# A four-layer transformer backward kernel: operands fetched one part ahead at the stage joints, some transposes moved to TensorE, one reordering on VectorE

## Chip, cores and metric

The kernel runs on one core of one Trainium2 chip, in one launch. The metric is the device time of that launch in microseconds (us), lower is better. A core has TensorE (PE in the profile, its weight loads PEld), VectorE (DVE), ScalarE (ACT), GpSimd (POOL), the sync engine SP, which here only issues DMAs, and 16 DMA engines.

## What is computed

Four residual layers alternate between linear attention (A, layers 0 and 2) and attention in a sliding window of 256 (B, layers 1 and 3), with the same weights for both A layers and for both B layers. The kernel returns the output x4 and, by back-propagation of `grad_out`, the gradients of x and of four weight matrices. Cut to what matters:

```python
def A(x, wqkv, wo):                       # x: [1, 2048, 640], 32 heads of 20
    q, k, v = split(x @ wqkv)             # wqkv: [640, 1920]
    pq, pk = phi(q), phi(k)               # phi(t) = (t + 1 if t > 0 else exp(t)) + 1e-6
    kv, z = pk^T v, sum(pk)               # per head
    return (pq kv) / (pq z + 1e-6) @ wo
def B(x, wqkv, wo):
    s = mask(q k^T / sqrt(20))            # 0 <= i - j < 256
    return softmax(s) v @ wo
x = x + A(ln(x)); x = x + B(ln(x)); x = x + A(ln(x)); x = x + B(ln(x))
out, vjp = jax.vjp(f, A_x, A_wqkv, A_wo, B_wqkv, B_wo)
return out, *vjp(grad_out)
```

## The kernel before

Rows are cut into 16 tiles of 128; the 640 columns are 5 tiles of 128; the 32 heads form 8 groups of 4. After the forward part (until about 875 us) come these stages:

- `seg_attention_bwd(3)` (about 875 to 1205 us): the backward pass of the softmax of layer 3, over 128 units (group, row tile). A unit makes scores twice (L905), e = exp (ACT, L919), dS = e times dP (DVE, two halves, L939), needs dS transposed, and five units later forms dq, dk, dv by products (L965), evicted into `dqkv_o` (L998) and stored to the DRAM tensor `dqkv` by POOL. Half 0 of dS is transposed by a DMA (`self.tr`, from SP's queue), half 1 by TensorE (`flip`, L949) through the one PSUM buffer `tp`, evicted by ACT and DVE in turn.
- `seg_dense_bwd(3)`, part 1 (to about 1349): per row of layer 3, dh = dqkv W^T (L773, needs `dqkvT`, the DMA-transposed row), LayerNorm backward on ACT and DVE (`ln_bwd`, L776 to L790), which ends with the residual gradient `car` (L790); then for linear-attention layer 2, car transposed (L730), dO = g Wo^T (L738), the products `do_o` on POOL (L753) and their row sums `do_s` on DVE (L755), dN, its transposes, dq (`dq_t`, L1256), and sums over all rows in two PSUM banks ("bands"). `close_A_bwd` turns the bands into the block-diagonal matrix `dmbd`, cleared before by POOL (L1151), and its transpose `dmbdT`.
- part 2 (to about 1499): per row dk and dv from `pk_ld`, `pkT`, `vT` (a load and two DMA transposes; `dkdv`), the products with WA^T, LayerNorm backward, and the slab dO of layer 1 (`B_do`).
- `seg_attention_bwd(1)` (to about 1967), with the weight gradients of layers 3 and 2 filled in; `seg_dense_bwd(1)`, part 1 (to about 2111) and part 2 (to about 2219).
- `wgrad` for layer 1 and then 0 (to the end): four jobs of 4, 2, 4 and 2 chunks of columns. Each output tile sums 16 matmuls (L1388), and `wg_o` (L1394) adds the part of the earlier layers, `wg_pt`.

The order of the work: the program is written row by row as a list of small functions with an offset in rows (`plan`); a scheduler orders instructions of each engine by dependences and priorities, and a pool's number of buffers bounds how far it runs ahead. `self.queue` and `queue2` hold loads that `drip` puts out on SP a few at a time, kept in the order of the program; SP issues in order, so what stands behind a DMA that waits, waits too. `behind` adds an order between two instructions without a semaphore. The loads of dense backward (`rows_in`, `tr`), the dS transposes, wgrad's loads and its output stores are all in SP's queue; other stores go out on POOL (`flush`). Lines that set the offsets:

```python
plan = ((fetch, 2), (dh0, 0), (dh1a, 0), (flip_g, -1), (dh1b, 0), (flip_dN, -2), (dO, -1), (flip_dq, -3), (dq_band, -2))  # part 1
plan = ((fetch, 4), (fetch2, 2), (dh0, 0), (flip_dkv, 1), (dh1a, 0), *tail[:1], (dh1b, 0), *tail[1:2], (dkdv, 2), *tail[2:])  # part 2
for s in range(-4, TT + 2):
```

Of the kernel before, what the change touches and what calls it, by code (L numbers as in the profile page):

```python
# [16 lines left out]
P = 128  # L17
DH = 20
# [5 lines left out]
class Kern:  # L24

    def __init__(self, ctx, tc, x0, A_wqkv, A_wo, B_wqkv, B_wo, grad_out, outs):
# [14 lines left out]
        self.queue, self.queue2, self.stores = [], [], []  # L41
        self.x0, self.grad_out = x0, grad_out
# [121 lines left out]
    def load_w(self, pool, kind, name):  # L164

        D, DT = self.D, self.DT
        if name == "W":
            t = pool.tile([P, DT, self.QT], BF, name=f"W{kind}")
            src = self.Wqkv[kind].rearrange("(kt p) n -> p kt n", p=P)
            pairs = [(t[:, k, c:c + D], src[:, k, c:c + D]) for c in range(0, self.QT, D) for k in range(DT)]  # L170
# [572 lines left out]
    def do_scaled(self, l, tt, ps, o, dst, pw):  # L743
# [11 lines left out]
        nc.vector.tensor_reduce(out=s, in_=self.hv(t), axis=AX.X, op=ALU.add, negate=True)  # L755
# [20 lines left out]
    def ln_bwd(self, l, tt, ps, hn, g, pw):  # L776
# [13 lines left out]
        nc.vector.scalar_tensor_tensor(out=self.car[:, tt, :], in0=u, scalar=ab[:, 0:1], in1=g,  # L790
                                       op0=ALU.add, op1=ALU.add)
# [65 lines left out]
    def seg_attention_bwd(self, l, fill, end):  # L857
# [5 lines left out]
        JL, PL, OH, WG = 5, 1, 4, 12 * DH  # L863
        units = [(g, b) for g in range(G) for b in range(TT)]
        slabs, e_of, ds_of, dsT_of = {}, {}, {}, {}
        self.att_outs, self.att_step = {}, 0
        with ExitStack() as st:
# [63 lines left out]
            def dscore(u, half, ps):  # L931
# [10 lines left out]
                if half == 0:  # L942
                    self.tr(dsT_of[u][:, 0:2 * nkt, :], ds_of[u][:, 0:2 * nkt * P])

            def flip(u):
                nb = 2 * span(units[u][1])[1]
                tp = ps_o.tile([P, 1024], BF, name="tp")
                for i in range(nb):
                    nc.tensor.transpose(tp[:, i * P:(i + 1) * P], ds_of[u][:, (nb + i) * P:(nb + i + 1) * P],  # L949
                                        self.ident)  # L950
                dst = dsT_of[u][:, nb:2 * nb, :].rearrange("p i q -> p (i q)")
                evac(u + 1)(dst, tp[:, 0:nb * P])
# [56 lines left out]
            n = len(units)  # L1009
            for s in range(n + JL):  # L1010
# [16 lines left out]
                if 0 <= b2 < n:  # L1027
                    dscore(b2, 1, pb)
                if bank:
                    job(s - JL, *bank)  # L1030
# [116 lines left out]
    def close_A_bwd(self, bands, pool, pt):  # L1147

        nc, D, DT, H = self.nc, self.D, self.DT, self.H
        dmbd = pool.tile([P, DT, 6 * P], BF, name="dmbd")  # L1150
        nc.gpsimd.memset(dmbd, 0.0)  # L1151
# [12 lines left out]
        return dmbd, dmbdT  # L1164
# [7 lines left out]
    def seg_dense_bwd(self, l, w, mid):  # L1172
# [5 lines left out]
        with ExitStack() as st:  # L1178
# [4 lines left out]
            dqT = pb.tile([P, DT, self.T], BF, name="dqT")  # L1183
            rows = lambda t: slice(t * P, (t + 1) * P)

            with ExitStack() as s2:
# [4 lines left out]
                WTA = WoTB = None  # L1191
                pps = self.pool(s2, "ps", 2, PSUM)
                pbd = self.pool(s2, "psb", 1, PSUM)
# [7 lines left out]
                def fetch(t):  # L1201
# [7 lines left out]
                    o[t] = self.rows_in(pl.tile([P, D], BF, name="o_ld", bufs=4), self.o_d[a][:, t, :])  # L1209
                    pq[t] = self.rows_in(pl.tile([P, D], BF, name="pq_ld", bufs=5), self.tm(sv["pq"])[:, t, :])  # L1210
# [27 lines left out]
                def dq_band(t):  # L1238
# [16 lines left out]
                    dq[t] = p1w.tile([P, D], BF, name="dq_t")  # L1255
# [4 lines left out]
                def flip_dq(t):  # L1260
                    self.flip(dq.pop(t), DT, dqT[:, :, rows(t)], pt, [nc.scalar.copy])

                plan = ((fetch, 2), (dh0, 0), (dh1a, 0), (flip_g, -1), (dh1b, 0), (flip_dN, -2), (dO, -1), (flip_dq, -3),
                        (dq_band, -2))
                for s in range(-2, TT + 3):
                    for f, d in plan:
                        if 0 <= s + d < TT:
                            f(s + d)
                    self.drip(2)
                    if s == 2:  # L1270
                        WTA = self.load_w(pb, 0, "WT")
                        WoTB = self.load_w(pb, 1, "WoT") if a > 0 else None
                dmbd, dmbdT = self.close_A_bwd(bands, pb, pt)
            mid()

            with ExitStack() as s2:
                p2 = self.pool(s2, "b2")
# [3 lines left out]
                hn, o, pk, pkT, vT, ps, gT, dkv, dkvT = ({} for _ in range(9))  # L1281
# [3 lines left out]
                def fetch(t):  # L1285
                    pk[t] = self.rows_in(pl.tile([P, D], BF, name="pk_ld"), sv["pk"][rows(t), :])
                    pkT[t] = pl.tile([P, DT, P], BF, name="pkT")
                    self.tr(pkT[t], sv["pk"][rows(t), :])
                    vT[t] = pl.tile([P, DT, P], BF, name="vT")
                    self.tr(vT[t], sv["v"][rows(t), :])  # L1290
# [6 lines left out]
                def dkdv(t):  # L1297
                    f = pw.tile([P, D], BF, name="dphi")
                    nc.vector.tensor_scalar(out=f, in0=pk.pop(t), scalar1=-1e-6, scalar2=1.0, op0=ALU.add, op1=ALU.min)
# [13 lines left out]
                    vT.pop(t), pkT.pop(t)  # L1313
# [34 lines left out]
                for s in range(-4, TT + 2):  # L1348
# [11 lines left out]
    def wgrad(self, l, pools, first=False):  # L1360

        nc, TT, D, DT, HD = self.nc, self.TT, self.D, self.DT, self.HD
        kind = l % 2
        pW, pw = pools[:2]
        jobs = [(self.hn_d[l], self.dqkv_d[l], 480, self.part[kind][0], (self.out_dWA, self.out_dWB)[kind], kind == 1),
                (self.o_d[l], self.g_d[l], HD, self.part[kind][1], (self.out_dWoA, self.out_dWoB)[kind], False)]
        for lhs_d, rhs_d, w, part, out, perm in jobs:
            lhs = pW.tile([P, TT, D], BF, name="wg_l", bufs=2)
            self.later([(lhs[:, tt, :], lhs_d[:, tt, :]) for tt in range(TT)])
            n = part.shape[1] // w  # L1370

            def load(c):
                r = pw.tile([P, TT, 480], BF, name="wg_r")
                return r, [(r[:, t:t + 2, 0:w], rhs_d[:, t:t + 2, c * w:(c + 1) * w]) for t in range(0, TT, 2)]
            rhs, pieces = load(0)
            self.later(pieces)
            if first:
                yield
            self.drip(len(self.queue), False)
            for c in range(n):  # L1380
                nxt, pieces = load(c + 1) if c + 1 < n else (None, [])
                for m in range(DT):
                    rows = slice(m * P, (m + 1) * P)
                    pt = pw.tile([P, 480], F32, name="wg_pt")
                    self.dma(pt[:, 0:w], part[rows, c * w:(c + 1) * w], nc.sync)
                    ps = pools[2].tile([P, 512], F32, name="wg")[:, 0:w]
                    for tt in range(TT):
                        nc.tensor.matmul(ps, lhsT=lhs[:, tt, rows], rhs=rhs[:, tt, 0:w],  # L1388
                                         start=(tt == 0), stop=(tt == TT - 1))
                        yield  # L1390
                        if tt % 8 == 7 and pieces:
                            self.dma(*pieces.pop(0), nc.sync)
                    o = pw.tile([P, 480], BF, name="wg_o")
                    nc.vector.tensor_add(o[:, 0:w], ps, pt[:, 0:w])  # L1394
                    if perm:
                        for h in range(w // (12 * DH)):
                            g = c * (w // (12 * DH)) + h
                            dst = out[rows, :].rearrange("r (t g c) -> r t g c", t=3, c=4 * DH)[:, :, g, :]
                            self.dma(dst, o[:, h * 12 * DH:(h + 1) * 12 * DH].rearrange("p (t c) -> p t c", t=3),
# [147 lines left out]
```

## Time and profile before

| | |
|---|---|
| time, median of 3 runs | 2412.37 us (2407.59 to 2415.21) |
| the profiled execution | 2408.5 us, of which the span is 2406.8 |
| TensorE clock granted, mean | 0.935 |
| busy: PE, DVE, ACT, POOL | 2141.7, 1550.2, 1259.9, 1156.0 us |
| DMA | 472 MB, 196 GB/s over the span |
| TensorE idle in 1205 to 1499 (dense 3) | 33.6 us |
| in 1499 to 1967 (attention 1) | 46.5 us |
| in 1967 to 2219 (dense 1) | 26.7 us |
| in 2219 to 2407 (wgrad) | 11.2 us |

The profiled execution is 3.9 us under the median. "Busy" is the time in which an engine executes; the idle times are the stretch less TensorE's busy time in it. A line of a timeline gives the start in us, the length, the engine (PEld is TensorE's weight load, SPq an issue in SP's queue), the line of the kernel, the operation with output and input, the shapes, the number of instructions drawn together and, in brackets, the idle time before them and what ended it. The granted clock is a share of full speed[...].

### The profile page before, as it was taken

To read this page: it belongs to the slowest core of one execution; us is meant where nothing else is said; L and a number is where in the kernel's file an instruction comes from. 1 tells how busy PE (TensorE), PEld (TensorE's weight loads), DVE (VectorE), ACT (ScalarE), POOL (GpSimd) and SP (SyncE) were. 2 spreads that over 40 slices of the span, in tenths; PEclk is the share of its full clock that TensorE was granted. 3 is DMA by queue.
4 is the path that set the end of the run, shared out by engine and by line. 5 is a ranking of instruction groups with operands and counts; after the bars stand their busy time and mean duration, and the time that the engine had idled before them with its cause. 6 is when DMAs were issued, how large, how long until landed. Compare 5 with 4: busy or idle time off the path is not lost. (4 is left out here: it accounts for less than half of the span.)

```text
span 2406.8 us, 68820 instructions
## 1 busy us (share of the span) xinstructions
PE 2141.7 (89%) x27566; PEld 1491.8 (62%) x27672; DVE 1550.2 (64%) x2991; ACT 1259.9 (52%) x2002; POOL 1156.0 (48%) x1791
## 2 busy tenths in 40 slices
PE   6879899879998689999989797889999979889989
PEld 4645565545555357777667575667777747657445
DVE  6657777557778558878766586556667656646112
ACT  4447777637777557777623353555666633333000
POOL 4447667656877535656533243445555533311000
PEclk9989999989999859999899898789999989989999
DMA  8599898478998798889998695999889898497797
GB/s 257 145 185 217 183 198 185 132 175 197 226 209 187 190 242 163 147 149 164 181 230 200 166 241 172 241 211 198 178 177 209 169 211 226 122 266 207 204 272 213
DMA packets 813666, 472.08 MB, mean 196 GB/s; under 512 B 609664, under 2 KB 780336, under 8 KB 813344
## 3 DMA queue, kind: packets, MB, share of 16 engines
q1 hardware_dynamic: 771152, 334.46, 67.0%
q0 software_dynamic: 42192, 133.21, 17.9%
q8 instruction: 216, 3.54, 0.6%
q14 instruction: 106, 0.87, 0.1%
HBM read 187.07 MB, written 161.19 MB: 145 GB/s over the span
## 5 line engine op out<-in xcount | busy, mean ns | idle before, releaser
L939 DVE SCALAR_TENSOR_TENSOR ds<-sp,e 128x768 bf16<-128x768 f32 (+2 forms) x512 | 462.8, 906 | 235.5 <-PE sp L905 148.9
L919 ACT ACTIVATE e<-sp 128x768 bf16<-128x768 f32 (+2 forms) x512 | 395.0, 776 | 257.4 <-PE sp L905 172.0
L418 ACT ACTIVATE e<-s 128x1024 bf16<-128x1024 f32 x360 | 365.2, 1025 | 109.2 <-PE s L412 67.2
L412 PE MATMUL s<-qbd,ring 128*128 128x512 bf16 x614 | 212.3, 388 | 7.7 <-ACT e L418 3.9
L1045 PEld LDWEIGHTS <-wg_l 128*128 128x128 bf16 x2800 | 187.3, 99 | 45.6 <-DVE wg_o L1051 14.1
L923 POOL TENSOR_SCALAR_AFFINE_SELECT e<-e 128x512 bf16<-128x512 bf16 x256 | 164.6, 643 | 94.0 <-ACT e L919 91.4
L905 PE MATMUL sp<-KT,QT 32*128 32x384 bf16 (+2 forms) x1024 | 184.8, 345 | 17.6 <-ACT e L919 10.5
L421 POOL TENSOR_SCALAR_AFFINE_SELECT e<-e 128x512 bf16<-128x512 bf16 x256 | 170.0, 666 | 54.1 <-ACT e L418 52.5
L905 PE MATMUL sp<-VT,dOT 32*128 32x384 bf16 (+2 forms) x1024 | 180.9, 341 | 10.8 <-ACT e L919 7.2
L1388 PE MATMUL wg<-wg_r,wg_l 128*128 128x480 bf16 (+1 forms) x960 | 176.8, 347 | 7.4 <-DMA out_dram<-wg_o 6.4
L1045 PE MATMUL acc<-wg_r,wg_l 128*128 128x160 bf16 x1840 | 157.4, 239 | 24.3 <-DMA wg_l<-o 7.4
L267 PE MATMUL d<-W,ln_hnT 128*128 128x320 bf16 x960 | 150.0, 304 | 28.3 <-ACT ln_hnT L732 9.6
L368 PE MATMUL d<-W,ln_hnT 128*128 128x480 bf16 x640 | 158.5, 380 | 4.0 <-DMA ln_hnT<-ln_hn 1.3
L424 POOL TENSOR_SCALAR_AFFINE_SELECT e<-e 128x512 bf16<-128x512 bf16 x224 | 150.9, 674 | 9.9 <-ACT e L418 9.1
L1388 PEld LDWEIGHTS <-wg_l 128*128 128x128 bf16 x960 | 94.5, 99 | 89.5 <-DMA out_dram<-wg_o 6.7
L773 PE MATMUL d<-WT,dqkvT 128*128 128x320 bf16 x960 | 144.4, 304 | 4.5 <-DMA dqkvT<-dqkv 4.5
L440 PEld LDWEIGHTS <-e 128*128 128x128 bf16 x2880 | 110.4, 97 | 60.5 <-POOL e L421 18.5
L927 POOL TENSOR_SCALAR_AFFINE_SELECT e<-e 128x512 bf16<-128x512 bf16 x224 | 142.8, 638 | 0.0
L267 PEld LDWEIGHTS <-ln_hnT 128*128 128x128 bf16 x960 | 93.8, 99 | 78.0 <-issue 22.5
L949 PE MATMUL tp<-ident,ds 128*128 128x128 bf16 x1440 | 135.9, 234 | 5.3 <-DVE ds L939 3.3
L440 PE MATMUL d<-v_slab,e 128*128 128x42 bf16 (+1 forms) x2880 | 115.9, 180 | 23.1 <-POOL e L421 16.1
L965 PEld LDWEIGHTS <-dsT 128*128 128x128 bf16 x2880 | 93.5, 98 | 67.5 <-issue 46.4
(204 smaller groups left out, 4554.0 us busy)
## 6 DMA issues: line engine op xcount, KB each, us to landing
qkvT<-ring POOLq DMA_DIRECT2D x32, 512.0 KB, 5.1
dqkv<-dqkv_o POOLq DMA_DIRECT2D x64, 240.0 KB, 4.2
wg_r<-dqkv SPq DMA_DIRECT2D x64, 240.0 KB, 4.6
hn<-ln_hn SPq DMA_DIRECT2D x64, 160.0 KB, 3.0
qk<-qk_flat POOLq DMA_DIRECT2D x64, 160.0 KB, 3.9
qk_r<-qk SPq DMA_DIRECT2D x32, 320.0 KB, 4.5
hn_ld<-hn SPq DMA_DIRECT2D x64, 160.0 KB, 3.6
dqkv<-dkv_t POOLq DMA_DIRECT2D x32, 320.0 KB, 4.0
```

The lines of the kernel that those rows point to most:

```text
L267: nc.tensor.matmul(ps, lhsT=hnT[:, k, :], rhs=W[:, k, ci * HD:(ci + 1) * HD], start=(k == 0), stop=(k == self.DT - 1))
L368: nc.tensor.matmul(ps, lhsT=hnT[:, k, :], rhs=W[:, k, ci * 480:(ci + 1) * 480], start=(k == 0), stop=(k == self.DT - 1))
L412: nc.tensor.matmul(ps[:, i, :], lhsT=self.ring_at(ring, 1, kt)[:, g, :], rhs=self.qbd[b % 2][:, g, :, :], start=True, stop=True)
L418: nc.scalar.activation(e[:, 0:i + 1], ps[:, 0:i + 1], ACT.Exp, scale=self.c_att)
L421: nc.gpsimd.affine_select(out=ev, in_=ev, compare_op=ALU.is_ge, fill=0.0, base=0, pattern=[[0, 4], [1, P]], channel_multiplier=-1)
L440: nc.tensor.matmul(ov[:, h % 16:h % 16 + w, :], lhsT=ev[i][:, hh, :], rhs=v[:, h:h + w, 0:DH + 1], start=(i == 0), stop=(i == nkt - 1), sk ...
L905: nc.tensor.matmul(ps[:, j, 0:nkt * P], lhsT=slabs[g][ta][r0:r0 + HP, b * P:(b + 1) * P], rhs=slabs[g][tb][r0:r0 + HP, k0 * P:(k0 + nkt) * P],
L919: nc.scalar.activation(ev[:, 2 * half:2 * half + 2], ps[:, :, 0:nkt * P].rearrange("p h (i k) -> p h i k", k=P), ACT.Exp, scale=c_att)
L923: nc.gpsimd.affine_select(out=ev[:, :, nkt - 1, :], in_=ev[:, :, nkt - 1, :], compare_op=ALU.is_ge, fill=0.0, base=0, pattern=[[0, 4], [-1 ...
L939: nc.vector.scalar_tensor_tensor(out=dv[:, hs], in0=ps[:, :, 0:nkt * P].rearrange("p h (i k) -> p h i k", k=P), scalar=c_att, in1=ev[:, hs ...
L1045: x = self.nc.tensor.matmul(ps[:, 0:w], lhsT=lhs(t), rhs=rhs(t), start=(t == 0), stop=(t == self.TT - 1), skip_group_check=True)
L1388: nc.tensor.matmul(ps, lhsT=lhs[:, tt, rows], rhs=rhs[:, tt, 0:w], start=(tt == 0), stop=(tt == TT - 1))
```

## The change

It has eight parts.

1. `do_s` (L755) is ordered behind the last written `car` (`self.car_ins`, L790).
2. The pieces of W are loaded in the column order D, 2D, 0 in place of 0, D, 2D.
3. For layer 1, the last 8 units' half 0 of dS is transposed on TensorE by `flip(u, 0)`, and not by DMA: 8 DMA transposes fewer, 48 TensorE transposes and 8 evictions (4 on ACT, 4 on DVE) more.
4. `dmbd` is taken from the outer pool and cleared by DVE at the start of `seg_dense_bwd`, not by POOL; `dmbdT` has a pool of its own, and the band banks are opened ahead of the pool `ps` and closed by hand.
5. `pk_ld`, `pkT` and `vT` of rows 0 to 2 are fetched by `fetch_kv` in the last steps of part 1, into a pool that both parts share. In the order of SP's instructions these nine DMAs stand around rows 4 to 6 of part 1.
6. In part 1, `o_ld` and `pq_ld` are fetched one row later (`fetch2`), with 3 and 4 buffers in place of 4 and 5; `dq_t` comes from another pool.
7. Part 2's loop starts at step -2, not -4: two steps of `drip` fewer.
8. `wgrad` is one generator over the chunks of all four jobs. It loads the next chunk's right-hand side also across jobs, and the next job's left-hand side during the first chunk of a job, a piece after every third matmul (before: every eighth); its 80 output stores are issued by POOL.

```diff
-            pairs = [(t[:, k, c:c + D], src[:, k, c:c + D]) for c in range(0, self.QT, D) for k in range(DT)]
+            pairs = [(t[:, k, c:c + D], src[:, k, c:c + D]) for c in (D, 2 * D, 0) for k in range(DT)]
...
-        nc.vector.tensor_reduce(out=s, in_=self.hv(t), axis=AX.X, op=ALU.add, negate=True)
+        x = nc.vector.tensor_reduce(out=s, in_=self.hv(t), axis=AX.X, op=ALU.add, negate=True)
+        if self.car_ins is not None:
+            self.behind(x, self.car_ins)
...
-        nc.vector.scalar_tensor_tensor(out=self.car[:, tt, :], in0=u, scalar=ab[:, 0:1], in1=g,
+        self.car_ins = nc.vector.scalar_tensor_tensor(out=self.car[:, tt, :], in0=u, scalar=ab[:, 0:1], in1=g,
...
+        FLIP = 8 if l == 1 else 0
...
-                if half == 0:
+                if half == 0 and u < n - FLIP:
                     self.tr(dsT_of[u][:, 0:2 * nkt, :], ds_of[u][:, 0:2 * nkt * P])
-            def flip(u):
+            def flip(u, half=1):
                 nb = 2 * span(units[u][1])[1]
+                c = half * nb
                 tp = ps_o.tile([P, 1024], BF, name="tp")
                 for i in range(nb):
-                    nc.tensor.transpose(tp[:, i * P:(i + 1) * P], ds_of[u][:, (nb + i) * P:(nb + i + 1) * P],
+                    nc.tensor.transpose(tp[:, i * P:(i + 1) * P], ds_of[u][:, (c + i) * P:(c + i + 1) * P],
                                         self.ident)
-                dst = dsT_of[u][:, nb:2 * nb, :].rearrange("p i q -> p (i q)")
-                evac(u + 1)(dst, tp[:, 0:nb * P])
+                dst = dsT_of[u][:, c:c + nb, :].rearrange("p i q -> p (i q)")
+                evac(u + half)(dst, tp[:, 0:nb * P])
...
                     dscore(b2, 1, pb)
+                if n - FLIP <= b2 < n:
+                    flip(b2, 0)
...
-        dmbd = pool.tile([P, DT, 6 * P], BF, name="dmbd")
-        nc.gpsimd.memset(dmbd, 0.0)
...
+            dmbd = pb.tile([P, DT, 6 * P], BF, name="dmbd")
+            nc.vector.memset(dmbd, 0.0)
             rows = lambda t: slice(t * P, (t + 1) * P)
+            plA = self.pool(st, "b2a", 3)
+            psb = st.enter_context(ExitStack())
+            pk, pkT, vT = {}, {}, {}
+            def fetch_kv(t):
+                pk[t] = self.rows_in(plA.tile([P, D], BF, name="pk_ld"), sv["pk"][rows(t), :])
+                pkT[t] = plA.tile([P, DT, P], BF, name="pkT")
+                self.tr(pkT[t], sv["pk"][rows(t), :])
+                vT[t] = plA.tile([P, DT, P], BF, name="vT")
+                self.tr(vT[t], sv["v"][rows(t), :])
...
+                pbd = self.pool(psb, "psb", 1, PSUM)
                 pps = self.pool(s2, "ps", 2, PSUM)
-                pbd = self.pool(s2, "psb", 1, PSUM)
...
-                    o[t] = self.rows_in(pl.tile([P, D], BF, name="o_ld", bufs=4), self.o_d[a][:, t, :])
-                    pq[t] = self.rows_in(pl.tile([P, D], BF, name="pq_ld", bufs=5), self.tm(sv["pq"])[:, t, :])
+                def fetch2(t):
+                    o[t] = self.rows_in(pl.tile([P, D], BF, name="o_ld"), self.o_d[a][:, t, :])
+                    pq[t] = self.rows_in(pl.tile([P, D], BF, name="pq_ld", bufs=4), self.tm(sv["pq"])[:, t, :])
...
-                plan = ((fetch, 2), (dh0, 0), (dh1a, 0), (flip_g, -1), (dh1b, 0), (flip_dN, -2), (dO, -1), (flip_dq, -3),
-                        (dq_band, -2))
+                plan = ((fetch, 2), (fetch2, 1), (dh0, 0), (dh1a, 0), (flip_g, -1), (dh1b, 0), (flip_dN, -2), (dO, -1),
+                        (flip_dq, -3), (dq_band, -2))
...
+                    if TT - 2 <= s < TT + 1:
+                        fetch_kv(s - TT + 2)
...
-                dmbd, dmbdT = self.close_A_bwd(bands, pb, pt)
-            mid()
...
+                pT = self.pool(s2, "b2t")
+                dmbdT = self.close_A_bwd(bands, dmbd, pT, pt)
+                psb.close()
+                mid()
...
                 def fetch(t):
+                    if t not in pk:
+                        fetch_kv(t)
...
-                for s in range(-4, TT + 2):
+                for s in range(-2, TT + 2):
...
+        chunks = [(j, c) for j, job in enumerate(jobs) for c in range(job[3].shape[1] // job[2])]
...
+        for i, (j, c) in enumerate(chunks):
+            _, _, w, part, out, perm = jobs[j]
+            pieces = load_rhs(i + 1) if i + 1 < len(chunks) else []
+            if c == 0 and j + 1 < len(jobs):
+                pieces = pieces + load_lhs(j + 1)
...
-                        if tt % 8 == 7 and pieces:
+                    if tt % 3 == 2 and pieces:
...
-                        self.dma(out[rows, c * w:(c + 1) * w], o[:, 0:w], nc.sync)
+                    self.dma(out[rows, c * w:(c + 1) * w], o[:, 0:w], nc.gpsimd)
```

## Prediction

> **What bounds the kernel now.** I read the page first, then a table of busy time by stage, then TensorE's timeline at each place where one stage hands over to the next. From the page:
>
> ```profile
> PE 2141.7 (89%) x27566; PEld 1491.8 (62%) x27672; DVE 1550.2 (64%) x2991; ACT 1259.9 (52%) x2002; POOL 1156.0 (48%) x1791
> ...
> PE   6879899879998689999989797889999979889989
> ...
> PEclk9989999989999859999899898789999989989999
> ```
>
> TensorE is busy 89% of the span. Of the lower digits of its row, those of slices 21, 23, 25, 26, 33, 36 and 39 (one slice is 60.2 us) lie where backward stages meet; most of the others are in the forward part, which the change all but leaves alone. No other engine is over 64%. So a gain has to come from TensorE's idle time at these joints, and from the clock it loses there. The stages that the change edits (columns: stretch, its length, busy us of PE, PEld, DVE, ACT, POOL with counts, granted clock, DMA share, GB/s):
>
> ```profile
> 1205.00:1349.00 144.00, 127.67 (x1221) 95.05 (x1221) 92.03 (x182) 49.65 (x83) 51.91 (x53) 0.96 0.78 190
> ...
> 1499.00:1967.00 468.00, 421.55 (x7896) 326.85 (x7896) 290.67 (x440) 267.14 (x443) 237.38 (x393) 0.92 0.98 199
> ...
> 2111.00:2219.00 108.00, 96.92 (x872) 72.39 (x871) 63.59 (x123) 36.91 (x64) 16.43 (x30) 0.94 0.95 250
> ```
>
> TensorE's timeline in windows at the joints; in brackets the idle time before and what ended it:
>
> ```profile
> 1213.16 5.09 PE L773 MATMUL d<-WT,dqkvT 128*128 128x320 bf16 x24 [4.53 <-DMA dqkvT<-dqkv]
> ...
> 1225.62 0.45 PE L730 MATMUL t<-ident,car 128*128 128x128 bf16 x5 [1.37 <-DVE car L790]
> ...
> 1354.94 0.49 PE L798 MATMUL d<-dmbd,pkT 128*128 128x140 bf16 x6 [2.08 <-DMA pkT<-pk]
> ...
> 1374.42 1.49 PE L773 MATMUL d<-WT,dqT 128*128 128x320 bf16 x5 [2.60 <-DVE dO_t L747]
> ...
> 1953.52 0.56 PE L965 MATMUL acc<-qk_r,dsT 128*128 128x40 bf16 x12 [7.38 <-DMA dsT<-ds]
> ...
> 1978.93 0.69 PE L730 MATMUL t<-ident,car 128*128 128x128 bf16 x5 [4.71 <-issue]
> ...
> 2034.56 0.45 PE L730 MATMUL t<-ident,car 128*128 128x128 bf16 x5 [0.26 <-DVE car L790]
> ...
> 2116.34 0.76 PE L798 MATMUL d<-dmbd,pkT 128*128 128x140 bf16 x6 [4.67 <-DMA vT<-v]
> ...
> 2313.55 16.68 PE L1388 MATMUL wg<-wg_r,wg_l 128*128 128x480 bf16 x67 [6.36 <-DMA out_dram<-wg_o]
> ```
>
> Each bracket names an operand that came late: a transposed dqkv row, pk and v rows, the last dS tiles, the next right-hand side. In the SP queue's timeline the 7.38 has its cause, and the first lines of POOL and DVE in dense backward 3 show a second kind of delay:
>
> ```profile
> 1940.90 6.55 SPq L152 DMA_TRANSPOSE dqkvT<-dqkv  x1
> ```
>
> ```profile
> 1210.97 3.30 POOL L1151 MEMSET dmbd<- 128x3840 bf16 x1 [3.59 <-DMA dqkv<-dqkv_o]
> ...
> 1211.38 3.07 DVE L1254 TENSOR_SCALAR dphi<-pq_ld 128x640 bf16<-128x640 bf16 x1 [5.30 <-DMA pq_ld<-pq]
> ```
>
> The transpose that holds SP for 6.55 us has the dS transposes queued behind it; the dphi that usually takes 0.33 us takes 3.07 under POOL's memset.
>
> [...] after the 3.45 us gap that ends at 1334.44, ten L738 matmuls take 2.83 us, and 1.52 in steady rows. So a gap costs more than its length. [...] the best 14 to 15 us stretches here show 341, a long one (2314 to 2360) 299, and I use the latter.
>
> **The change part by part.** The sum is against the profiled run, 2408.5 us (span 2406.8), which lies 3.9 under the median 2412.4.
>
> *Order of W's columns.* The start waits for the third row of car, which is issued after all 15 pieces in either order: 0.
>
> *Residual gradient ahead of row sums.* In a row of part 1 (7.78 us from dq_t to dq_t) DVE runs dh_u, waits 1.29 for POOL's do_o, then do_s (0.82), then car (0.88), for which TensorE waits 0.26. With car ahead of do_s it ends over 1 us earlier, and the wait goes: 0.26 x 13 steady rows x 2 layers = 6.8; I take 6.5. What is late next is dN: its cast follows do_s, and its transposes start 1.07 us after it now (2034.59 to 2035.66). In the new order (dh_u, dq_t, car, do_s, dphi, cast) the cast ends at about the same time, since dq_t fills DVE's wait for POOL: slack about 0.8. Nothing then waits.
>
> *Joint into dense backward (3 and 1): o_ld and pq_ld a row later, memset on DVE.* Two loads fewer stand ahead of the second dqkvT: 2 x 0.48 = 0.96 of the 4.53. The memset no longer slows dphi, so the 1.37 goes. On DVE it is one instruction of 1920 words: between 1.0 (three times the 0.33 of a 128x640 bf16 pass) and 2.7 us (three times a 0.89 f32 pass); it waits for the same store of dqkv_o as POOL did, with the first dh_junk behind it, which the d matmuls keep waiting anyway. Layer 3: 2.5 (0 to 5).
>
> *pk, pkT and vT of three rows fetched in part 1, part 2 begun two steps later.* In layer 3, from the close of the bands (1349.67) to the first d matmul of row 3 (1383.57) are 33.9 us. TensorE's work in them, busy time times clock from the table, is 7.06 x 0.81 + 11.75 x 0.99 + 9.58 x 0.86 = 25.6. If no operand is late, 8.3 go, and car's 0.7 at the end of part 1: 9 (3 to 12). In layer 1, 2111.36 to 2146.30 are 34.9, with 5.04 x 0.66 + 11.0 x 0.87 + 9.26 x 0.87 = 21.0 of work: 13.9. There, however, the DMA share is 1.1 for 70 us after the joint, and SP issues 5.7 us per row of 5.8; I take 11 (3 to 15). The nine fetches are not free: the instruction order of the changed kernel has them in SP's queue already around rows 4 to 6 of part 1, about 3 x (0.4 + 1.2 + 1.25 + gaps) = 9 us of issue ahead of dqkvT of rows 5 and 6. The lead of those transposes is some 4 to 10 us: cost 1, up to 10 for both layers.
>
> *Last dS tiles of layer 1 on TensorE.* The waits that go: 7.38 + 3.52 + 1.35 in the tail, and most of the 4.71, since the d matmuls start earlier while the loads of row 0 are there (2 fewer ahead). With them goes clock: L738 takes 2.85 and the 8 L773 2.14 at 1980 to 1985, about 2.4 too much, and some 2 in the tail. Sum 21. Against it 48 transposes (8 x 0.5 to 0.82 = 4.0 to 6.6 on TensorE), and 4 of the 8 evictions on DVE (0.55 each, 2.2), where DVE already sets the pace of the tail at some 2.4 us a unit; the single transpose buffer makes both halves take turns. Net 12 (6 to 16).
>
> *Joint into attention backward 1.* The order of DVE gives about 1.5, but the fourth load of dO's transposes now heads SP's queue ahead of qk_r, dO_r and wg_r (10 x 0.45 behind it), and the first e still waits for the last dOT_ring store: 0 (-3 to +3).
>
> *Final weight gradients.* Idle 0.26 + 0.42 + 0.35 + 6.36 and some 3 of clock (the first 42 of the 480-wide matmuls 11.62 us, 8.4 warm) = 10.4. SP no longer waits for wg_o ahead of a load, as the 80 stores go to POOL, which is idle there. But one job, 10 x 2.33 = 23.3 us of matmuls, has to be fed with some 8.3 MB for itself and the next: 27.8 us at 299 GB/s, so 4.5 stay: gain 6 (0 to 10).
>
> Sum: 6.5 + 2.5 + 9 + 11 - 1 + 12 + 0 + 6 = 46. 2408.5 - 46 = 2362.5, or 2366 from the median. I say **2363 us**.
>
> **Rivals.** *B: supply is the bound.* The edits move transfers, they do not remove them, but for eight transposes. If the queues set the pace, part 2 of layer 1 keeps 3 of 11, layer 3 6 of 9, weight gradients 0, and the hoisted fetches cost 4: 6.5 + 2.5 + 6 + 3 - 4 + 11 + 0 + 0 = 25, so 2385. For it: DMA share 0.95 over that stage, and SP's 5.7 of 5.8 us. Against it: the share falls to 0.16 in 2089 to 2100, just ahead of the joint, so there is room earlier. *C: the change doesn't do what it says.* Scheduled elsewhere, the fetches meet the same landing times, and the flips cost what the waits did; the row's 6.5 alone stays: 2402. Against it: the changed order does have fetches and flips ahead. *D, slower: dN becomes the late operand.* do_s is put behind car in all 26 steady rows of part 1 and some 14 of layer 3's part 2, and a PE transpose waits for what follows it. At x us per row it costs 40x against 46: it decides from x = 1.15, which needs the cast about 2 us later than I work out. At 1.5 (a full op of 0.82 more, twice over): 2408.5 - 46 + 60 = 2422. For it: the order on DVE is the one edit that acts in every row; against it: the 0.8 of slack and a row's 1.15 us of DVE idle.
>
> **How the numbers follow.** About 0.3% (7 us) is what a measurement of this kernel can tell from no change. Forecast 0.60 (its own range 2345 to 2376), B 0.24, C 0.07, D 0.09. Faster: 0.60 + 0.24 + a part of C (which straddles 2405) = 0.86; same 0.05; slower 0.09. The range reaches from the forecast with half of its terms at their good ends (2342) to B with the fetches at their full cost and the flips at their worst (2398); it leaves out D, most of C and a little of the forecast's low side.
>
> **What would show it.** Right: in the changed profile no `<-DMA dsT` wait in the last 15 us of attention 1 and dense 1's first car transposes earlier by about 12 us relative to its start; no pkT or vT wait in the first three rows of part 2; rows of 7.5 us without a car wait; stores of wg_o on POOL and a wait under 5 us near the third quarter of the weight gradients. Wrong: waits on dqkvT in rows 4 to 7 of part 1, on vT in rows 5 to 10 of part 2, on dN or do_slab in every row, or on tp evictions in the tail.

## The result, and the profile after

The changed kernel takes 2372.24 us (median of 4 runs, 2367.87 to 2374.75) where the kernel before takes 2413.79 beside it (4 runs, 2407.59 to 2415.55): a ratio of 0.983, 95% interval 0.9805 to 0.9856, 41.6 us less. The forecast was 2363, range 2342 to 2398. The profiled execution of the changed kernel is its slowest of the four, 2374.75 us with a span of 2373.0, so the two profiled spans differ by 33.8 only. Where a number below depends on that, it says so.

The page after, the lines that answer to those shown of before:

```profile
PE 2141.4 (90%) x27720; PEld 1493.3 (63%) x27720; DVE 1552.4 (65%) x2997; ACT 1262.9 (53%) x2006; POOL 1200.3 (51%) x1869
...
PE   6879999879998779999989898789999989989989
...
PEclk9989999979999859999899999789999999999999
```

TensorE's busy time is the same to 0.3 us; POOL's has grown by 44: some 51 for the 80 stores of the weight gradients, less two memsets of 3.3. So nothing was computed less; waits went. TensorE's timeline of the changed kernel at the places of the prediction (lines are 1 to 26 further down in its code):

```profile
1216.42 5.92 PE L776 MATMUL d<-WT,dqkvT 128*128 128x320 bf16 x30 [2.06 <-DMA dqkvT<-dqkv]
...
1347.95 0.73 PE L731 MATMUL t<-ident,dkv_t 128*128 128x128 bf16 x10 [0.30 <-DVE dkv_t L1325]
...
1361.94 0.84 PE L776 MATMUL d<-WT,dqT 128*128 128x320 bf16 x5 [0.17 <-DVE dO_t L748]
...
1943.00 0.53 PE L971 MATMUL acc<-qk_r,dsT 128*128 128x40 bf16 x12 [0.45 <-ACT dqkv_o L1004]
...
1959.40 0.71 PE L731 MATMUL t<-ident,car 128*128 128x128 bf16 x5 [4.93 <-DVE car L793]
...
2033.77 0.44 PE L731 MATMUL t<-ident,car 128*128 128x128 bf16 x5
...
2122.57 0.33 PE L801 MATMUL d<-dmbdT,vT 128*128 128x140 bf16 x3 [1.35 <-DMA vT<-v]
...
2270.42 2.33 PE L1414 MATMUL wg<-wg_r,wg_l 128*128 128x320 bf16 x16 [1.33 <-DVE wg_o L1420]
...
2274.39 2.33 PE L1414 MATMUL wg<-wg_r,wg_l 128*128 128x320 bf16 x16 [1.63 <-DVE wg_o L1420]
```

Four kinds of waits are gone or nearly so: for car in every row, for pkT and vT and for dO_t (0.17 us is left) where part 2 of dense 3 begins, for dsT at the end of attention 1. Three are not. In part 2 of dense 1 vT still ends waits (1.35 us above, up to 2.99). Behind attention 1, 4.93 stands where 4.71 stood, now with VectorE's car as its end; and the 6.36 us of the weight gradients have become seven waits of 0.49 to 1.63, together 6.49.

The stages, each from the start of its first line on TensorE to the start of the next one's (us, one profile each). Attention ends with its last product, the last stretch with the kernel; "car n" is the transpose of the n-th row's car on TensorE, counted from 0. The columns e1 to e15 are experiments of the next section: e1 has the reordering alone, e5 lacks the program's prefetch, e13 also its pool, and e15 keeps the reordering, the pools and part 6.

| stretch | before | after | e1 | e5 | e13 | e15 |
|---|---|---|---|---|---|---|
| forward, to attention 3 | 827.2 | 830.9 | 834.5 | 831.0 | 830.1 | 829.7 |
| attention 3 | 378.4 | 378.7 | 376.4 | 378.5 | 381.1 | 381.4 |
| its end to car 1 of dense 3 | 20.0 | 18.9 | 19.2 | 17.8 | 17.2 | 19.2 |
| car 1 to car 15 | 108.8 | 102.4 | 102.4 | 103.7 | 102.9 | 102.4 |
| car 15 to car 1 of part 2 | 45.2 | 34.9 | 44.3 | 34.6 | 44.4 | 35.2 |
| part 2, car 1 to car 15 | 109.2 | 108.0 | 108.0 | 108.0 | 108.0 | 108.0 |
| to attention 1 | 10.5 | 10.5 | 10.5 | 10.5 | 10.1 | 10.5 |
| attention 1 | 468.2 | 459.5 | 464.4 | 454.2 | 458.8 | 465.9 |
| its end to car 1 of dense 1 | 20.3 | 23.8 | 19.6 | 22.7 | 23.7 | 17.4 |
| car 1 to car 15 | 109.0 | 102.4 | 102.4 | 102.4 | 102.4 | 102.4 |
| to the bands' close | 14.5 | 14.3 | 14.8 | 14.8 | 14.7 | 14.8 |
| to the first weight-gradient matmul | 107.6 | 100.9 | 107.6 | 97.9 | 102.9 | 95.6 |
| weight gradients | 187.8 | 187.9 | 184.0 | 186.0 | 186.0 | 185.7 |

With car ahead of do_s, the rows of dense backward 1 take 102.4 in all thirteen profiles; those of dense 3 take 102.4 to 103.7. The forward part varies from 819.4 to 834.5 over the fourteen kernels profiled here, which differ in it by nothing but W's column order, and attention 1 by 14. So a change of a few us in a whole time can't be laid to an edit; I read the stretch that the edit acts on, and a few us are uncertain there too, as each stretch comes from one profile.

### The profile page after: what moved, and what is told of

Its sections match the earlier page's. It is cut to its first block, busy times and chain, and to the rows that moved or that the text cites. A ratio compares the mean times of both kernels' runs of the same rounds, so it can differ in the third digit from the quotient of the medians.

```text
span 2373.0 us, 69090 instructions
## 1 busy us (share of the span) xinstructions
PE 2141.4 (90%) x27720; PEld 1493.3 (63%) x27720; DVE 1552.4 (65%) x2997; ACT 1262.9 (53%) x2006; POOL 1200.3 (51%) x1869
## 4 chain that ended last, share of the span: by engine, by line
PE 41%; DMA 7%; issue 6%; DVE 3%; SPq 2%; ACT 2%; POOL 1%; POOLq 0%; DVEq 0%; ACTq 0%
PE d L776 10%; PE acc L971 7%; PE acc L1052 7%; PE sp L910 5%; PE tp L955 3%; PE d L739 3%; PE t L731 2%; PE wg L1414 2%; SPq L126 1%; DVE ds L944 1%; DMA dsT<-ds 1%; ACT e L924 1%; PE d L801 1%; DMA dqkvT<-dqkv 1%; DMA pq1w<-wg_o 1%
## 5 line engine op out<-in xcount | busy, mean ns | idle before, releaser
L413 PE MATMUL s<-qbd,ring 128*128 128x512 bf16 x720 | 242.1, 387 | 4.8 <-ACT e L419 2.5
L910 PE MATMUL sp<-VT,dOT 32*128 32x384 bf16 (+2 forms) x1024 | 179.4, 339 | 10.5 <-ACT e L924 6.3
L1414 PE MATMUL wg<-wg_r,wg_l 128*128 128x480 bf16 (+1 forms) x960 | 174.9, 344 | 8.4 <-DVE wg_o L1420 8.4
L1052 PE MATMUL acc<-wg_r,wg_l 128*128 128x160 bf16 x1840 | 155.7, 238 | 19.6 <-DMA wg_l<-o 6.1
```

The lines of the kernel that those rows point to most:

```text
L413: nc.tensor.matmul(ps[:, i, :], lhsT=self.ring_at(ring, 1, kt)[:, g, :], rhs=self.qbd[b % 2][:, g, :, :], start=True, stop=True)
L910: nc.tensor.matmul(ps[:, j, 0:nkt * P], lhsT=slabs[g][ta][r0:r0 + HP, b * P:(b + 1) * P], rhs=slabs[g][tb][r0:r0 + HP, k0 * P:(k0 + nkt) * P],
L1052: x = self.nc.tensor.matmul(ps[:, 0:w], lhsT=lhs(t), rhs=rhs(t), start=(t == 0), stop=(t == self.TT - 1), skip_group_check=True)
L1414: nc.tensor.matmul(ps, lhsT=lhs[j][:, tt, rows], rhs=rhs[i][:, tt, 0:w], start=(tt == 0), stop=(tt == TT - 1))
```

## The experiments

**One edit alone: car ahead of do_s (e1).**

```diff
 # the kernel before, and only:
+        self.car_ins = None
...
+        x = nc.vector.tensor_reduce(out=s, in_=self.hv(t), axis=AX.X, op=ALU.add, negate=True)
+        if self.car_ins is not None:
+            self.behind(x, self.car_ins)
...
-        nc.vector.scalar_tensor_tensor(out=self.car[:, tt, :], in0=u, scalar=ab[:, 0:1], in1=g,
+        self.car_ins = nc.vector.scalar_tensor_tensor(out=self.car[:, tt, :], in0=u, scalar=ab[:, 0:1], in1=g,
```

> The kernel before with part 1 of the change alone: do_s ordered behind car. My theory: the row of part 1 falls from 7.78 us to the 7.35 of the changed kernel by this edit alone, in both layers, 2 x 6.4 = 13 us, and the row of layer 3's part 2 by at most 0.1 (1.3 in all); time about 13 us under before, stages outside dense backward as before. Rival: the row is shorter because loads and memset were moved (SP and POOL are freer); then the row stays at 7.6 to 7.8 and the time within 5 us of before. Rival D of the prediction: TensorE waits for dN; then a row over 7.8.

2388.0 us against 2407.1 beside it (0.9917, 0.9893 to 0.9942), 19 less in the medians. The rows take 102.4 in both layers, to the tenth those of the changed kernel: 6.4 + 6.6 = 13.0 us belong to this edit, and so do the 1.2 by which the rows of part 2 became shorter (108.0 here too). The rest of the 19 is not explained: attention 1 and the weight gradients, which the edit doesn't touch, are 3.8 shorter each in this profile, and the forward part is 7.3 longer. A row before and the same place in e1, TensorE's timelines:

```profile
2030.88 3.42 PE L773 MATMUL d<-WT,dqkvT 128*128 128x320 bf16 x24
```

```profile
2020.21 3.42 PE L776 MATMUL d<-WT,dqkvT 128*128 128x320 bf16 x24
2023.47 0.44 PE L731 MATMUL t<-ident,car 128*128 128x128 bf16 x5
```

From the start of the 24 matmuls to car's transposes are 3.26 us; before they were 3.68 (2030.88 to 2034.56). The difference is 0.42, though the bracket there said 0.26: without a wait the transposes start 0.16 before the drawn end of the matmuls (2020.21 + 3.42 = 2023.63), and the bracket counts from that end.

**The pools, not the place in the program (e5, e13).** First the prefetch was undone in the program:

```diff
-                    if TT - 2 <= s < TT + 1:
-                        fetch_kv(s - TT + 2)
...
-                for s in range(-2, TT + 2):
+                for s in range(-4, TT + 2):
```

> The changed kernel without fetch_kv in part 1 and with part 2 begun at step -4 (parts 5 and 7 undone). My theory: from the last row of part 1 to the second car of part 2 in layer 3 it takes 45 us again and not 34.9, and layer 1's part 2 some 107 and not 97 to 101, together 14 to 18 us more; the nine fetches ahead of dqkvT of rows 5 and 6 cost nothing, since the rows stay at 102.4 per 14. Rival: the joint is short because the memset, the pools and the DVE order changed; then the joint stays under 38.

Both parts of my expectation failed: the joint took 34.6, as short as ever, and layer 1's part 2 97.9. The time was 2368.0 (0.9814, 0.976 to 0.9869). By what I had written the rival won, but it named the memset, the pools and VectorE's order in one. SP's timeline of e5 shows which of them to look at:

```profile
1230.25 0.42 SPq L126 DMA_DIRECT2D pk_ld<-pk  x1
...
1237.64 0.58 SPq L126 DMA_DIRECT2D pk_ld<-pk  x1
```

The fetches that the program asks for in part 2 are issued between the dqkvT transposes of rows 4 and 6 of part 1, as in the changed kernel. So I moved only their pool back into part 2:

```diff
-            plA = self.pool(st, "b2a", 3)
...
                 p2w = self.pool(s2, "b2w", 2)
+                plA = self.pool(s2, "b2a", 3)
```

> The kernel of e5 with the pool of pk_ld, pkT and vT opened inside part 2 again, as before the change. In e5 the program asked for these rows only in part 2, and yet the joint stayed short (34.6 us in layer 3), because the scheduler put the first nine fetches around rows 4 to 6 of part 1 all the same. My theory now: what lets them go early is that their pool has memory of its own; with memory that part 1 has to give back first, they stand behind all of dqkvT in SP's queue, the joint in layer 3 takes 44 to 45 us and layer 1's part 2 104 to 108, together some 17 us more than e5, about 2385 in time. Rival: the nearer car (part 1 of the change), the memset or the PSUM banks made the joint short; then it stays under 38.

2385.0 us (0.9883, 0.9835 to 0.9931). The joint of layer 3 is back at 44.4, as long as in e1. Layer 1's part 2 takes 102.9, 5.0 over e5, but only 2.0 over the changed kernel, and under the 104 to 108 that I expected. SP issues the first of these loads only when part 1 ends, and TensorE's old waits are there again:

```profile
1340.98 0.33 SPq L126 DMA_DIRECT2D pk_ld<-pk  x1
```

```profile
1351.00 0.49 PE L801 MATMUL d<-dmbd,pkT 128*128 128x140 bf16 x6 [1.71 <-DMA pkT<-pk]
...
1352.74 0.33 PE L801 MATMUL d<-dmbdT,vT 128*128 128x140 bf16 x3 [0.99 <-DMA vT<-v]
...
1370.41 1.49 PE L776 MATMUL d<-WT,dqT 128*128 128x320 bf16 x5 [2.56 <-DVE dO_t L748]
```

In layer 3, memory of its own for these tiles makes the joint short; fetch_kv in part 1 and the later start of the loop add nothing that can be seen. In layer 1 the pool accounts for a part only: with it undone, part 2 is still 4.7 shorter than the 107.6 of before and of e1, and no run shows why. The whole times of e5 and e13 have intervals that overlap; the stretches decide.

**Car, the pools and part 6, without the rest (e15).**

```diff
 # the changed kernel, with:
-        FLIP = 8 if l == 1 else 0
+        FLIP = 0
...
-            nc.vector.memset(dmbd, 0.0)
+            nc.gpsimd.memset(dmbd, 0.0)
 # the fetches' place and the loop as in e5; wgrad and W's order as before
```

> Of the change only part 1 (car first), the pool of its own for pk, pkT and vT with the places that make room for it, and part 6; no flips, weight gradients, W's order, memset (on POOL) and the program's place of the fetches as before. My theory: these give nearly the whole gain, 13 + 10 + 8 us, that is 2378 to 2386 where the kernel before takes 2410 to 2414; the rest (flips 4 to 8 less what the joint gives back) is what it lacks. Rival: parts 3, 4 and 8 matter; then it is over 2390.

2368.2 us (0.9821, 0.9779 to 0.9863): below the range that I gave, and not apart from the changed kernel. Parts 2, 3, 7, 8, the memset and the fetches' place bring together nothing that a time can show.

**The flips (e4).**

```diff
-        FLIP = 8 if l == 1 else 0
+        FLIP = 0
```

> The changed kernel with half 0 of the last 8 units' dS transposed by DMA again (part 3 undone). My theory: the flips saved 15 us of waits for dsT in the tail and cost 4 on the way, and 3.5 were lost again behind attention 1; so attention 1 takes 466 to 472 us and not 459.5, the joint behind it 19 to 21 and not 23.8, the time rises by 5 to 9. Rival: the waits for dsT went because fewer other DMAs stand in SP's queue in the changed kernel; then attention 1 stays under 463.

Attention 1 took 460.2 and the time was 2373.0 (0.9833, 0.9798 to 0.9868), no rise at all, so by what I had written the rival won. But its waits for dsT are back, in TensorE's timeline:

```profile
1926.00 0.56 PE L971 MATMUL acc<-qk_r,dsT 128*128 128x40 bf16 x12 [5.53 <-DMA dsT<-ds]
...
1933.66 0.55 PE L971 MATMUL acc<-qk_r,dsT 128*128 128x40 bf16 x12 [3.49 <-DMA dsT<-ds]
...
1939.28 0.55 PE L971 MATMUL acc<-qk_r,dsT 128*128 128x40 bf16 x12 [2.13 <-DMA dsT<-ds]
```

The whole stage was the wrong ruler. Call the tail what lies between the last `wg_o` of the weight gradients filled into attention 1 and its last product. There e4 takes 33.0 us, the changed kernel 27.0 (34.9 before); the part ahead of it, which the edit hardly touches, varies from 427 to 440. To car 1 of dense 1 it is 54.7 against 50.8; a pair with the memset on POOL (e15 and e8, which differ in other parts as well) gives 50.6 against 46.2. So the flips gain about 4 us where they act. One profile for each, with 46.5 to 51.1 over six kernels with flips and the memset on DVE: the sign is fairly sure, the size is not.

**The joint behind attention 1 (e2, e12, e8).** VectorE in the changed kernel:

```profile
1949.35 1.66 DVE L1190 MEMSET dmbd<- 128x1920 uint32 x1 [5.12 <-DMA dqkv<-dqkv_o]
...
1953.03 0.33 DVE L1273 TENSOR_SCALAR dphi<-pq_ld 128x640 bf16<-128x640 bf16 x1 [0.71 <-DMA pq_ld<-pq]
...
1957.30 0.33 DVE L1273 TENSOR_SCALAR dphi<-pq_ld 128x640 bf16<-128x640 bf16 x1 [3.86 <-DMA pq_ld<-pq]
...
1958.45 0.88 DVE L793 SCALAR_TENSOR_TENSOR car<-dh_u,dh_ab,g_ld 128x640 bf16<-128x640 f32 x1
```

The second dphi, of row 1, stands ahead of car of row 0 and waits 3.86 us for a load that the change fetches a row later. SP at the same place:

```profile
1925.90 11.37 SPq L153 DMA_TRANSPOSE dqkvT<-dqkv  x2
...
1941.38 4.92 SPq L126 DMA_DIRECT2D mbdT<-mbdT  x5
1946.47 0.34 SPq L126 DMA_DIRECT2D hn_ld<-hn  x1
```

The two transposes of dqkvT hold SP for 11.37 us, eleven weight loads follow, and the first load of row 0 comes 2.7 us after attention's last product (1943.8), where before it came at once. So the prefetch of rows 0 and 1 was brought back (e2), and then more weight loads put ahead of the two transposes (e12):

```diff
+                    if t < 2:          # in fetch(t); e2 and e12
+                        fetch2(t)
...
+                    if t in o:         # in fetch2(t)
+                        return
...
-                self.drip(3 if s < TT or s >= n - TT else 2)
+                self.drip(3 if s < TT else 5 if s >= n - TT else 2)      # e12
```

> The changed kernel with o_ld and pq_ld of rows 0 and 1 alone fetched with their row again (part 6 undone for these two rows). My theory: at the start of dense backward 1 of the changed kernel DVE stands 3.86 us at dphi of row 1, which waits for pq_ld and stands ahead of dh_u and car of row 0, so TensorE idles 4.93; with the early loads this goes, and from the end of attention 1 to the second car transposes it takes 19 to 20 us and not 23.8, so about 4 us less in all, 0 to 1 in layer 3. Rival: car of row 0 is late because SP is still busy with WT, WoT and mbdT loads when attention ends (its hn_ld and g_ld come late too); then the stretch stays over 22.5.

> The changed kernel with the early pq_ld of e2 and five loads per step in place of three in the last 16 steps of attention, so that 15 of the weight loads stand ahead of the two dqkvT transposes in SP's queue and 7 behind them (9 and 11 in e2). My theory: after the tail was shortened, the start of dense backward 1 is set by SP, which issues its first hn_ld 2.7 us after attention's last product, as 11 weight loads stand behind transposes that wait for the last dqkv rows; with fewer of them behind, the first hn_ld comes at once, and the stretch from there to the second car takes 17 to 19 us (21.4 in e2, 23.8 in the changed kernel). Rival: the start is set by memory that attention frees or by the DMA engines; then it stays at 21 or more.

e2: from attention's end to car 1 21.4 us, between the theory's 19 to 20 and the rival's 22.5, with SP's first load 3.5 us behind the last product; 2367.1 (0.9833, 0.9793 to 0.9873). e12: 16.7, with that load 0.1 us behind; 2365.8 (0.9797, 0.9757 to 0.9837). The sizes are rough: e14 below has both edits too, and takes 19.9 with the load 1.2 us behind. SP's timeline of e12:

```profile
1944.98 2.42 SPq L126 DMA_DIRECT2D mbdT<-mbdT  x5
1948.92 0.32 SPq L126 DMA_DIRECT2D hn_ld<-hn  x1
```

Last, the memset alone went back to POOL (the memset line of e15's diff, e8):

> The changed kernel with the memset of dmbd on POOL again. My theory: the two joints into dense backward become longer by at most 1.5 us each, as dphi (3.1 us under the memset) stands ahead of dh_u and car; the time stays within 3 us of the changed kernel. Rival: the memset delays car of row 0 by its full 3.3 us in both layers, 5 to 7 us.

Both were wrong in sign for layer 1: from attention's end to car 1 it takes 19.3 us, 4.6 less than in the changed kernel (layer 3: 19.5 for 18.9); 2366.4 (0.9816, 0.9771 to 0.986). VectorE in e8:

```profile
1947.71 0.33 DVE L1273 TENSOR_SCALAR dphi<-pq_ld 128x640 bf16<-128x640 bf16 x1 [8.86 <-DMA pq_ld<-pq]
...
1949.94 0.89 DVE L793 SCALAR_TENSOR_TENSOR car<-dh_u,dh_ab,g_ld 128x640 bf16<-128x640 f32 x1
...
1952.01 0.33 DVE L1273 TENSOR_SCALAR dphi<-pq_ld 128x640 bf16<-128x640 bf16 x1 [1.19 <-DMA pq_ld<-pq]
```

Car stands ahead of the second dphi here: with the memset off VectorE the scheduler chose another order. The memset's 1.66 us were not the wait in the changed kernel (it ended at 1951.01, and the 3.86 came later), so the order is the likely cost; no run changes the order alone. Other kernels help to tell it from SP's backlog. With the second dphi ahead of car and the first load late by 1.5 to 3.0 us, the stretch is 22.7 to 23.9 (six kernels, the changed one among them). With that order and the load at 0.1 us it is 21.7 (e4), with e8's order and the load at 2.5 it is 19.3, with both good 17.4 (e15). So the order is worth some 4 us and the backlog about 2, from one profile each and with other edits between them.

**The weight gradients (e3, e6, e11).** e3 takes `wgrad` of before:

> The changed kernel with the weight gradients' code of the kernel before (part 8 undone). My theory: the stage is bound by the supply of its second job and takes 188 us either way, so the time is within 3 us of the changed kernel and the single wait of about 6 us comes back. Rival: part 8 gains its 6 us, and something else in the changed kernel (a cooler start, part 2's end) costs as much; then the stage takes 193 or more.

The stage takes 184.6 with the old code (one wait of 5.04 and one of 0.59), 187.9 with the new; 2366.4 (0.9825, 0.9801 to 0.985). With the old code it is 184.0 to 187.8 over four kernels, with the new 186.0 to 188.1 over seven (e6, e11 and e14 apart). Part 8 gains nothing, and may cost 1 to 2. Then six buffers for `wg_pt` (e6), and a kernel that leaves out the addition of the earlier layers' part and so its loads (e11):

```diff
-                pt = pw.tile([P, 480], F32, name="wg_pt")
+                pt = pools[3].tile([P, 480], F32, name="wg_pt")     # e6; pools[3]: 6 buffers
...
-                self.dma(pt[:, 0:w], part[rows, c * w:(c + 1) * w], nc.sync)     # e11
-                nc.vector.tensor_add(o[:, 0:w], ps, pt[:, 0:w])
+                nc.vector.tensor_copy(o[:, 0:w], ps)
```

> The changed kernel with six buffers for wg_pt in place of two. Seven waits of 0.5 to 1.6 us on wg_o in the second job of the weight gradients each follow a wait of DVE for wg_pt. Theory A, order in SP's queue: wg_pt is issued only when a buffer comes free and then stands behind 4 to 5 pieces of the next job; with six buffers these waits (6.5 us in sum) go and the stage takes about 182. Theory B, supply: the DMA engines are full in this job (share 1.03, 350 GB/s), so the wait moves to wg_l or wg_r and the stage takes 186 to 188.

> The changed kernel with the weight gradients' last stage leaving out the addition of the earlier layers' part: wg_pt isn't loaded and wg_o is a copy. Theory supply: the 13 MB of wg_pt in some 188 us are what the second job lacks; without them no wait on wg_o is left and the stage takes 178 to 181. Theory order (a load that stands behind others in SP's queue, whatever it brings): as wg_pt is the load that is late, its loss gives the same. What tells them apart is job by job: by supply the waits of the second job go to zero only if the DMA share there falls under 0.95; by order the share stays where it was and the waits still go. If the stage stays at 185 or more, both are wrong and it is the stores on POOL or the buffers of wg_o.

e6: the stage takes 184.6, between A's 182 and B's 186; 2360.3 (0.9808, 0.978 to 0.9835). The seven waits became two, and TensorE ran slower after the first: 16 matmuls take 3.19 us where they take 2.33 in the changed kernel, and the granted clock is 0.88 over 2237 to 2265.

```profile
2252.50 3.19 PE L1414 MATMUL wg<-wg_r,wg_l 128*128 128x320 bf16 x16 [2.33 <-DVE wg_o L1420]
2256.48 11.80 PE L1414 MATMUL wg<-wg_r,wg_l 128*128 128x320 bf16 x58 [0.80 <-DVE wg_o L1420]
```

e11: the stage takes 180.8, the kernel 2361.2 (0.9789, 0.9761 to 0.9818); waits of 2.70 in sum, DMA share 0.85 in the second job (2242 to 2267; 0.92 in the changed kernel). The table of busy time (columns as in the prediction) of the changed kernel, then of e11:

```profile
2252.00:2280.00 28.00, 21.50 (x151) 14.57 (x150) 4.42 (x9) 0.00 (x0) 5.80 (x11) 1.00 0.92 294
```

```profile
2242.00:2267.00 25.00, 22.30 (x163) 15.74 (x161) 5.08 (x10) 0.00 (x0) 6.32 (x11) 1.00 0.85 273
```

In the changed kernel 8.24 MB are moved in these 28 us. What `wg_o` itself waits for is on VectorE, in the changed kernel and then in e11:

```profile
2273.84 0.49 DVE L1420 TENSOR_TENSOR wg_o<-wg,wg_pt 128x320 bf16<-128x320 f32 x1 [3.48 <-DMA wg_pt<-po1w]
```

```profile
2264.10 0.49 DVE L1418 CAST wg_o<-wg 128x320 bf16<-128x320 f32 x1 [3.77 <-DMA out_dram<-wg_o]
```

So the second job waits for late loads of `wg_pt`: without them the stage is 7 us of 188 shorter, with more buffers for them 3. What is left in e11 ends with output stores, which give back the two buffers of `wg_o`; that was the third cause in my expectation. Whether the loads are late for want of bytes per us or for their place in SP's queue is not told apart by these two; the DMA share of the changed kernel was under 0.95 to begin with.

**All together (e14):** e12, e6, and the third job's left-hand side in a buffer of its own, loaded from the first job's third chunk on.

```diff
 # besides e12 and e6, and the third left-hand side's own buffer:
-            if c == 0 and j + 1 < len(jobs):
-                pieces = pieces + load_lhs(j + 1)
+            ahead = {0: 1, 2: 2, 6: 3}.get(i)
+            if ahead:
+                pieces = pieces + load_lhs(ahead)
```

> The changed kernel with what the runs suggest: pq_ld and o_ld of rows 0 and 1 early, five weight loads per step in the tail (e12), six buffers for wg_pt (e6), and a third buffer for the left-hand side of the weight gradients, so that the third job's is loaded from the third chunk of the first job on. Theory supply: the second job lacks operands only because left-hand side, right-hand side and parts of the next jobs all fall in its 23 us; spread over more of the first job its waits go, and the stage takes 179 to 182 (187.8 in the changed kernel, 184.6 in e6). Rival: buffers were not it, and the stage stays over 184. With 42 to 44 us from attention's last fill to the second car the time is about 2355, under the changed kernel by 12 to 18.

2363.8 us (0.9794, 0.975 to 0.9838). The stage takes 182.9, waits 3.78 in sum: most of the way to the 179 to 182 expected, and under the rival's 184. From the last fill to car 1 44.1. The ratio is the lowest of the kernels that compute everything, but its interval overlaps that of the changed kernel, and the gain of 12 to 18 over it is not shown: attention's part ahead of the tail took 439.9 in this profile, the longest of all.

## Why the prediction was right, and where it was not

By its own steps, against the two profiled spans (sum -33.8):

| step | forecast | measured |
|---|---|---|
| rows of part 1 | 6.5 | 13.0 |
| joint into dense 3 | 2.5 | 1.1 |
| part 1 to part 2, layer 3 | 9 | 10.3, and 1.2 in the rows after, which e1 has too |
| part 1 to part 2 and on, layer 1 | 11 | 7.0 |
| fetches in part 1's queue | -1 | 0: rows 102.4 in e1, without them, as after |
| flips and joint into dense 1 | 12 | 8.7 - 3.5 = 5.2 |
| joint into attention 1 | 0 | 0 |
| weight gradients | 6 | 0 |
| not touched (forward, attention 3) | 0 | -4.0 |

- *Rows*: the mechanism was right and the term too small by half. "TensorE waits 0.26" is the idle time behind the drawn end of a group, and without a wait the next group starts 0.16 ahead of that end (e1); the spacing of starts gave 0.43 a row (7.78 to 7.35). VectorE's order is the one worked out, though car takes 1.28 us there (2002.48 in the changed kernel, with POOL's do_o from 2001.18 to 2003.09), and 0.88 before (2033.62, where do_o had ended at 2032.86). dN did not become late: rival D needs a longer row, and there is none.
- *Joints between the parts*: the size was right for layer 3, with a slip in the sum: its windows (1349 to 1384) are 1.1 us longer than the stretch. Over the stretch itself TensorE's work is about 24.7 and not 25.6, which makes the forecast 9.9. In layer 1 it was 7.0 of 11 (7.0 to 11.7 in the other kernels with the pool outside). There rival B had a share: vT still ends waits of 1.35, 1.75 and 2.99 us in the first 60 us of part 2, which the prediction had named as a sign of short supply. My reason was half wrong: I laid it to the fetch in part 1 and to two steps fewer. e5 and e13 show that in layer 3 it is the pool's memory; in layer 1 that is some 2 to 5 us of it, and the rest stays open.
- *Memset and joint into dense backward*: "most of the 4.71" did not go. I took two loads fewer ahead of the transpose for a gain only, and did not look at what then stands at the head of VectorE's queue; and the shorter tail showed SP's backlog of weight loads. The DVE price lay between my bounds (1.66 in 1.0 to 2.7). The order of dphi and car could have been read from the changed kernel's instruction order.
- *Flips*: the waits for dsT went as worked out, but shorter ones (0.82, 1.53, 0.45) stand in the tail instead: TensorE's idle time there fell from 13.1 to 4.2, by 8.9 and not by 12.3, and the tail by 7.9, the cost of the flips in it included. The clock came back in part (0.75 to 0.89 in the tail), and not behind it (0.83 to 0.77, to car 1 of dense 1); the 4.71 did not go.
- *Weight gradients*: the estimate of 8.3 MB was right (8.24 measured), its consequence not. The waits left were 6.5 in that job, not 4.5, and 8.4 in the whole stage, where before they were 7.4. Of the 3 us of clock some 2 did come back (TensorE's busy time in the stage fell from 176.8 to 174.9); but the kernel ends 4.0 us behind the last `wg_o`, where before it was 3.0. Rival B's "weight gradients 0" was right for this stage alone.

Two readings of the prediction are off, though no term rests on them: slice 33 of TensorE's row is a 9 (35 is a low one), and the fastest stretch of 14 us moved 352 GB/s (2162 to 2176), not 341.

The stages that the change touches came to 37.8 of the 46: rows and the first joint were 9.0 more than forecast, the two joints of layer 1, the weight gradients and the joint into dense 3 some 18 less, and the fetches' cost of 1 did not come. The medians moved by 41.6. That the total came out near owes something to errors of both signs.

The prediction's example of lost clock is the gap of 3.45 us: behind it the granted clock of the kernel before is 0.50 (1334.4 to 1337.4), and ten L738 matmuls take 2.83 us there, where they take 1.52 at 1.00 (from 1320.32). It fell to 0.50 after shorter gaps too: 2.99 us in the changed kernel (2146.59 to 2149.46) and 2.33 us in e6 (2254 to 2260). As to the memset: under it on POOL (3.30 us) the first dphi took 3.07 and 3.16 us in the kernel before (layers 3 and 1); in layer 1 of e8 it took 0.33, as it came 0.2 us after the memset had ended. No two kernels here differ only in whether that dphi falls under the memset, so its cost is not measured apart.

## What to carry to other kernels

Where a scheduler orders a program, an early load needs memory that is not given back late; where the program asks for it mattered less here. Count a recurring wait by the spacing of starts in the two orders, not by the idle bracket. And when an edit takes the last wait of a stage away, look at the queue heads behind it: here the order of two instructions on VectorE, with a load fetched a row later, and SP's backlog gave back 3.5 of the 8.7 us that attention 1 had won.

## What was not expected of the hardware

The same forward part took 819.4 to 834.5 us from profile to profile, a spread of 0.6% of the whole time. And in two places a slower stretch of TensorE began some time after a gap had ended. After the 2.33 us of e6, which end at 2252.50, the granted clock is 0.95 until 2254 and 0.50 from there to 2260. After the gap of 2.99 us before 2144.62 of the changed kernel it is 1.00 until 2146.0, and ten matmuls that start at 2146.59 take 2.87 us at 0.50, where 1.52 at 1.00 is usual. So in both the first matmuls after the gap don't show the slower ones behind them. In the weight gradients of the changed kernel (2252 to 2280) the granted clock stayed at 1.00 through the gaps of 0.49 to 1.63 us: these cost no more than their length.
